# Regrouping the cluster products of an attention and MoE kernel, and moving its preparation work to other steps

## Chip, cores, metric

One core of a Trainium2 chip. The metric is the device time of one execution in microseconds (us), as the median of several executions; for one core there is no second die to compare, and every execution used here was with a granted TensorE clock of 0.994 to 1.0. The timed figure is about 1.9 us above the span of the profile of the same execution (311.12 beside 309.24 us). The one profile of the kernel before is of an execution of 311.12 us. Engines are named as in the profile: PE is TensorE (PEld its weight loads), DVE is VectorE, ACT is ScalarE, POOL is GpSimd, SP is SyncE.

## The reference

Attention over 4 batches x 8 heads x 768 positions x 64, in which a query sees only the keys of its own cluster, and then an MLP on the 3072 x 512 result:

```python
q_assign = argmax(einsum('bhsd,hcd->bhsc', q_n, c_n))     # 16 clusters for each head
k_assign = argmax(einsum('bhsd,hcd->bhsc', k_n, c_n))
scores = where(q_assign == k_assign, scale * q @ k.T, -1e9)
x = softmax(scores) @ v                                   # then to [3072, 512]
h = x @ w_in                                              # [3072, 2048]
g = h + sin(alpha * h)**2 / (alpha + 1e-9)
out = g @ w_out                                           # [3072, 512]
```

## The kernel before

Two heads make a "pair"; a batch has four pairs, and the 16 pairs are numbered through. A batch's attention has 48 steps. Each step issues one score block (`scores`), its exponential on ScalarE (`expo`), and, two or three steps behind, one block of probabilities times v (`pv`). Two PSUM areas hold the scores, so TensorE can be one block ahead of ScalarE and no more. One PSUM bank (OB) collects `pv`; at a pair's sixth block of a head VectorE normalises it, and the next `pv` has to wait for that.

The mask is made by one-hot rows that stand below q and k in the score matmul. For them TensorE forms, for each pair, the cluster scores (the *cluster product*, line 222), and VectorE makes the one-hot rows out of it in four pieces; DMAs on SP's queue put them in place:

```python
def prep_asn(m, part=0, parts=1, bk=None):        # the cluster product of pair m, float32
    ...
    for g in range(4):
        nc.tensor.matmul(
            out=s["asn"][32 * g : 32 * g + 32, ...],   # 32 columns of the array each
            lhsT=cnB[:, 2 * hp + g // 2, :],
            rhs=s["T32"][:, g, ...], start=True, stop=True)

def hot_steps(m, a):
    asn_at.add(a)
    at(a, lambda: (prep_asn(m), prep_hot(m, 0)))  # piece 0: 32x32 transposes out of PSUM
    at(a + 1, lambda: prep_hot(m, 1))             # 1: maximum of each 16
    at(a + 2, lambda: prep_hot(m, 2))             # 2: is_equal
    at(a + 3, lambda: (prep_hot(m, 3), prep_move(m)))   # 3: transposes back; 8 or 4 DMAs
```

Everything that is not attention's own work hangs in a plan by step. In batch 0 that is a lot: `prep_T` (three float32 transpositions on TensorE and a copy, four groups for each pair), `prep_D` (VectorE transposes for later pairs), `x_T` (transposition of a finished pair's result), casts and loads on GpSimd. In batches 1 to 3 the output matmuls of the batch before ("fillers") are dealt out over the steps:

```python
ahead = b == 0 and r % NJ == 1        # plan work goes ahead of pv at these steps of batch 0
if ahead:
    for fn in plan.get(i, []): fn()
for d in due.get(r, []): pv(base + d)
if not ahead:
    for fn in plan.get(i, []): fn()
if fill:
    fill.go((2 if r % NJ == 2 else 0 if r % NJ == 3 else 1) - (i in asn_at))
```

After the 48 steps comes the batch's MLP: for each of 16 blocks `hidden_mm` on TensorE into one of three PSUM areas, `snake` (sine on ScalarE, square on ScalarE or VectorE, multiply-add on VectorE into gT), and the first output matmuls with a lag of some blocks. `hidden_mm` of block f needs the area that `snake` of block f - 3 has read.

The softmax here doesn't subtract the row's maximum and nothing guards it: scores larger than these inputs give would overflow.

## Time and profile before

| | before |
|---|---|
| time, median of the first 3 runs | 312.74 us (311.97 to 312.76) |
| span of the profile | 309.2 us |
| TensorE busy | 300.7 us, 97% |
| ScalarE, VectorE, GpSimd busy | 238.8, 209.7, 141.1 us |
| cluster products | 15 of 8 matmul records, 120 records |

TensorE is nearly always busy, so a wait is not the usual cost here. What counts is how far apart the *starts* of its instructions lie: a duration in the timeline includes the pipeline's drain and overlaps the next one. For ScalarE, likewise, I give the period from one exponential's start to the next; "the period at step n" ends with the exponential of step n. It is 0.71 us when ScalarE is the bound; a longer one tells that TensorE was late with the scores.

### The profile page before, as it was taken

The numbers are of one execution on the slowest core, as the hardware profiler recorded it, in microseconds if no ns is written. First come the engines' busy times: TensorE is split into PE (matmuls) and PEld (weight loads), VectorE is DVE, ScalarE is ACT, GpSimd is POOL, SyncE is SP. The second block draws the span as 40 slices with busy tenths as digits, with TensorE's granted clock in tenths as the row PEclk, the third lists the DMA queues.
The fourth block names the chain that finished last, engine by engine and source line by source line (L and its number), as shares of the span: only waits on it lengthen the run. The fifth ranks groups of instructions, "written<-read, shape, count | busy, mean of one in ns | idle before, by whom it ended". The sixth has DMA issues, their size and how long they took to land.

```text
span 309.2 us, 7194 instructions
## 1 busy us (share of the span) xinstructions
PE 300.7 (97%) x2726; PEld 177.2 (57%) x2726; DVE 209.7 (68%) x369; ACT 238.8 (77%) x323; POOL 141.1 (46%) x231
## 2 busy tenths in 40 slices
PE   7899999999999999999999999999999999999995
PEld 3567666455455665555556656555556666555544
DVE  4786685899769876677867877677935313677721
ACT  5689987976598988687689998688679999687300
POOL 5789978048177199993006089970001090000000
PEclk9999999999999999999999999999999999999999
DMA  7548999999585477981054477420011021000031
GB/s 226 156 160 264 315 228 220 218 196 318 108 200 171 91 190 151 314 295 51 2 141 112 84 177 161 117 85 2 0 68 50 36 47 41 36 0 2 0 136 68
DMA packets 31105, 40.48 MB, mean 131 GB/s; under 512 B 5904, under 2 KB 24928, under 8 KB 31072
## 3 DMA queue, kind: packets, MB, share of 16 engines
q0 software_dynamic: 10240, 21.11, 26.3%
q1 hardware_dynamic: 20592, 18.87, 23.0%
q8 instruction: 21, 0.34, 0.5%
q14 instruction: 12, 0.10, 0.1%
q10 hardware_dynamic: 240, 0.06, 0.1%
HBM read 27.30 MB, written 6.29 MB: 109 GB/s over the span
## 4 chain that ended last, share of the span: by engine, by line
PE 90%; ACT 5%; DVE 3%; issue 1%; DMA 1%; SPq 0%; ACTq 0%; DVEq 0%
PE M L406 20%; PE S L437 18%; PE S L338 13%; PE OB L353 11%; PE M L437 8%; PE S L339 6%; PE OB L406 5%; PE M L222 3%; ACT pT L344 3%; PE S L406 2%; PE M L144 2%; DVE gT L462 1%; PE S L513 1%; DMA QK<-ohT 1%; PE M L377 1%
## 5 line engine op out<-in xcount | busy, mean ns | idle before, releaser
L344 ACT ACTIVATE pT<-S 128x768 bf16<-128x768 f32 x192 | 143.0, 810 | 16.7 <-PE S L339 15.6
L406 PE MATMUL M<-w_out_bf,gT 128*128 128x512 bf16 (+1 forms) x288 | 90.6, 373 | 0.0
L338 PE MATMUL S<-QK 80*128 80x512 bf16 x192 | 72.9, 380 | 2.1 <-ACT pT L344 1.3
L437 PEld LDWEIGHTS <-w_in_bf 128*128 128x128 bf16 x512 | 49.4, 98 | 38.4 <-issue 2.1
L353 PEld LDWEIGHTS <-pT 128*128 128x128 bf16 x1152 | 56.0, 97 | 21.7 <-DVE xs L365 0.7
L437 PE MATMUL S<-xT,w_in_bf 128*128 128x512 bf16 x352 | 66.2, 326 | 0.6 <-DVE gT L462 0.4
L353 PE MATMUL OB<-VX,pT 128*128 128x65 bf16 x1152 | 61.3, 193 | 0.3 <-DVE xs L365 0.3
L199 POOL TENSOR_SCALAR QK<-T 64x384 bf16<-64x384 f32 x80 | 43.4, 542 | 34.3 <-DMA T<-Tq 29.2
L450 ACT ACTIVATE s_sb<-S,alpha_col 128x768 bf16<-128x768 f32 (+2 forms) x45 | 39.7, 886 | 23.5 <-PE S L437 15.7
L406 PEld LDWEIGHTS <-gT 128*128 128x128 bf16 x400 | 39.0, 98 | 31.7 <-issue 6.5
L462 DVE SCALAR_TENSOR_TENSOR gT<-u_sb,ralpha,S 128x768 bf16<-128x768 bf16 (+2 forms) x45 | 44.7, 996 | 11.1 <-ACT u_sb L455 8.2
L339 PE MATMUL S<-QK 80*128 80x256 bf16 x192 | 51.9, 270 | 0.0
L399 POOL DMA_DIRECT2D xT<-xq x48 | 25.8, 546 | 28.2 <-DVE xq L391 27.2
L437 PE MATMUL M<-xT,w_in_bf 128*128 128x512 bf16 (+1 forms) x160 | 30.6, 326 | 0.0
L339 PEld LDWEIGHTS <-QK 80*128 80x128 bf16 x192 | 18.8, 98 | 17.6 <-issue 2.8
L458 DVE TENSOR_TENSOR u_sb<-s_sb 128x768 bf16<-128x768 bf16 (+2 forms) x41 | 23.9, 584 | 6.4 <-ACT s_sb L450 6.4
L211 POOL CAST VX<-v 128x768 bf16<-128x768 f32 x16 | 13.7, 855 | 31.6 <-issue 28.3
L364 DVE RECIPROCAL rec<-OB 128x6 f32<-128x6 f32 x32 | 6.1, 191 | 29.9 <-PE OB L353 29.9
L406 PE MATMUL OB<-w_out_bf,gT 128*128 128x512 bf16 (+1 forms) x80 | 26.2, 358 | 0.0
L450 ACT ACTIVATE s_sb<-M,alpha_col 128x512 bf16<-128x512 f32 (+1 forms) x40 | 20.9, 574 | 6.7 <-PE M L437 6.6
L462 DVE SCALAR_TENSOR_TENSOR gT<-u_sb,ralpha,M 128x512 bf16<-128x512 bf16 (+1 forms) x40 | 22.8, 611 | 4.8 <-ACT u_sb L455 4.4
L338 PEld LDWEIGHTS <-QK 80*128 80x128 bf16 x192 | 18.6, 97 | 6.8 <-issue 2.5
(84 smaller groups left out, 277.4 us busy)
## 6 DMA issues: line engine op xcount, KB each, us to landing
T<-Tq SPq DMA_DIRECT2D x80, 96.0 KB, 2.4
out_dram<-o_sb SPq DMA_DIRECT2D x23, 256.0 KB, 2.1
v<-in_v_dram POOLq DMA_DIRECT2D x14, 384.0 KB, 4.8
q<-in_q_dram POOLq DMA_DIRECT2D x13, 384.0 KB, 6.6
k<-in_k_dram POOLq DMA_DIRECT2D x13, 384.0 KB, 7.1
w_in_bf<-in_moe_w_in_dram POOLq DMA_DIRECT2D x4, 512.0 KB, 10.5
w_out_bf<-in_moe_w_out_dram POOLq DMA_DIRECT2D x4, 512.0 KB, 11.6
xT<-xq POOLq DMA_DIRECT2D x48, 24.0 KB, 2.2
```

What stands on the lines that cost most here:

```text
L199: nc.gpsimd.tensor_scalar(out=QK[0:D, m % NQK, h, t].rearrange("c (n i a) -> c i n a", i=4, a=32)[:, 2 * par : 2 * par + 2], in0=src[:, t] ...
L211: nc.gpsimd.tensor_copy(out=VX[m % NVX][:, :, :, 0:D], in_=st[m]["v32"])
L338: nc.tensor.matmul(out=dst[:, 0:512], lhsT=lhsT, rhs=T[:, 0, 0:512], start=True, stop=True)
L339: nc.tensor.matmul(out=dst[:, 512:S], lhsT=lhsT, rhs=T[:, 0, 512:S], start=True, stop=True)
L344: nc.scalar.activation(out=pT, in_=area(i)[:, 0:S], func=ACTF.Exp, scale=escale)
L353: nc.tensor.matmul(out=o3[:, j, :], lhsT=pT[:, P * j : P * j + P], rhs=VX[m % NVX][:, h, jof(m // NHP, kt), :], start=(kt == 0 and j == 0) ...
L399: nc.gpsimd.dma_start(out=xT[32 * g : 32 * g + 32, 0:2, QS * i : QS * i + QS], in_=xq[0].rearrange("p (h g n) -> p h g n", h=2, g=4)[32 * ...
L406: nc.tensor.matmul(out=bk[:, lo:hi], lhsT=gT[:, f, P * mt : P * mt + P], rhs=w_out_bf[:, f, lo:hi], start=(f == 0), stop=(f == NF - 1),)
L437: nc.tensor.matmul(out=ar[lo // 512][:, 0 : hi - lo] if isinstance(ar, tuple) else ar[:, lo:hi], lhsT=lhsT, rhs=xT[:, kk, :].rearrange("c ...
L450: nc.scalar.activation(out=s_sb[:, lo:hi], in_=src, func=ACTF.Sin, scale=alpha_col[:, f : f + 1])
L458: nc.vector.tensor_tensor(out=u_sb[:, lo:hi], in0=s_sb[:, lo:hi], in1=s_sb[:, lo:hi], op=ALU.mult)
L462: nc.vector.scalar_tensor_tensor(out=gT[:, f, lo:hi], in0=u_sb[:, lo:hi], scalar=ralpha[:, f : f + 1], in1=src, op0=ALU.mult, op1=ALU.add,)
```

## The change

It keeps every instruction and moves them. Neighbouring cluster products stand back to back (7-8, 10-11, 12-13, 14-15, and 4-5 in batch 0's MLP), the one-hot pieces of the second product of each late pair are put at steps where they come after the normalisation, batch 0's transpositions are spread anew, and GpSimd's v cast of pair 2 goes ahead of pair 3's second cast.

```diff
+    def hot_two(m, a, steps):
+        asn_at[a] = 2
+        at(a, lambda: (prep_asn(m), prep_asn(m + 1), prep_hot(m, 0), prep_hot(m + 1, 0)))
+        for n, (i, j, k) in enumerate(((a + 1, a + 2, a + 3), steps)):
+            at(i, lambda n=n: prep_hot(m + n, 1))
+            at(j, lambda n=n: prep_hot(m + n, 2))
+            at(k, lambda n=n: (prep_hot(m + n, 3), prep_move(m + n)))
 ...
-        (3, ((0, 14), (2, 16), (1, 17), (3, 18)), 20, (17, 19)),
-        (4, ((0, 22), (1, 24), (2, 28), (3, 30)), 32, (25, 31)),
-        (5, ((0, 34), (1, 36), (2, 40), (3, 41)), None, (37, 42)),
+        (3, ((0, 11), (1, 14), (2, 16), (3, 18)), 20, (16, 19)),
+        (4, ((0, 22), (1, 23), (2, 28), (3, 34)), None, (25, 35)),
+        (5, ((0, 32), (1, 38), (2, 40), (3, 42)), None, (39, 43)),
 ...
-    for g, i in enumerate((35, 37, 38, 39)):          # prep_D of pair 6
+    for g, i in enumerate((36, 39, 41, 41)):
-    for g, i in enumerate((42, 43, 44, 45)):          # prep_D of pair 7
+    for g, i in enumerate((44, 44, 46, 46)):
 ...
+    hot_one(6, ASTEPS + 8)
+    hot_one(9, ASTEPS + 32)
+    for m, b, r, steps in (
+        (7, 1, 20, (25, 26, 31)),
+        (10, 2, 2, (7, 8, 10)),
+        (12, 2, 32, (38, 41, 42)),
+        (14, 3, 2, (7, 8, 10)),
+    ):
+        hot_two(m, ASTEPS * b + r, [ASTEPS * b + i for i in steps])
 ...
-                at((23, 29, 46)[m], lambda m=m: x_T(m))
+                at((26, 30, 44)[m], lambda m=m: x_T(m))
 ...
-        own = [(1, OB, 3 if b else 4), (0, M0, 5 if b else 6)]
+        own = [(1, OB, 3 if b else 4), (0, M0, 5 if b else 7)]
 ...
+            if b == 0 and f == 1:
+                prep_asn(NHP, bk=OB)
+                prep_asn(NHP + 1, bk=M0)
+                prep_hot(NHP, 0)
 ... (the other one-hot pieces of pairs 4 and 5 after blocks 3 to 9; loads and casts of v)
```

More of the change, by code (lines that the diff above doesn't have):

```diff
@@ L575, in at, with hot_one @@
         plan.setdefault(i, []).append(fn)
-    asn_at = set()
-    def hot_steps(m, a):
-        asn_at.add(a)
+    asn_at = {}
+    def hot_one(m, a):
+        asn_at[a] = 1
         at(a, lambda: (prep_asn(m), prep_hot(m, 0)))
@@ L584, in hot_steps @@
         at(a + 3, lambda: (prep_hot(m, 3), prep_move(m)))
+    def hot_two(m, a, steps):
+        asn_at[a] = 2
+        at(
+            a,
+            lambda: (
+                prep_asn(m),
+                prep_asn(m + 1),
+                prep_hot(m, 0),
+                prep_hot(m + 1, 0),
+            ),
+        )
+        for n, (i, j, k) in enumerate(((a + 1, a + 2, a + 3), steps)):
+            at(i, lambda n=n: prep_hot(m + n, 1))
+            at(j, lambda n=n: prep_hot(m + n, 2))
+            at(k, lambda n=n: (prep_hot(m + n, 3), prep_move(m + n)))
     def pair_steps(m, make, asn, cast):
@@ L602, in prep_new @@
         at(k0 + 17, lambda: prep_cast(m, 1))
-        hot_steps(m, k0 + 8)
     for m, make, asn, cast in (
@@ L619 @@
         at(ASTEPS + 4 + 2 * h, lambda h=h: prep_cast(NHP + 3, h))
-    hot_steps(NHP + 2, ASTEPS + 8)
-    hot_steps(NHP + 3, ASTEPS + 14)
     for m, i in {4: 10, 5: 12, 6: 18, 7: 22}.items():
@@ L640 @@
                     at(2 * ASTEPS - 1, lambda m=m: load_qk(m, eng=nc.gpsimd))
+    hot_one(6, ASTEPS + 8)
[7 more added lines that the diff above has]
+        hot_two(m, ASTEPS * b + r, [ASTEPS * b + i for i in steps])
     for m in range(1, NP):
         if m > 1:
-            at(max(0, STEPS * m - (14 if m < 5 else 26)), lambda m=m: load_v(m, nc.gpsimd))
-        at(max(0, STEPS * m - (5 if m < 5 else 8)), lambda m=m: prep_v(m))
+            at(max(0, STEPS * m - (14 if m < 3 or m == 4 else 19 if m == 3 else 26)), lambda m=m: load_v(m, nc.gpsimd))
+        at(max(0, STEPS * m - (6 if m == 2 else 5 if m < 5 else 8)), lambda m=m: prep_v(m))
     for m in range(NP):
@@ L712 @@
             if fill:
-                fill.go((2 if r % NJ == 2 else 0 if r % NJ == 3 else 1) - (i in asn_at))
+                fill.go((2 if r % NJ == 2 else 0 if r % NJ == 3 else 1) - asn_at.get(i, 0))
         last = NHP * (b + 1) - 1
@@ L734 @@
                 fill.go(10 if f == 2 else 64, "act")
-            if b == 0 and f == 2:
-                prep_asn(NHP + 1, bk=M0)
-            if b == 0 and f in (6, 10):
-                prep_S(NHP + 2 + (f - 6) // 4)
-            if b == 0 and f in (3, 5, 7, 9):
-                prep_hot(NHP + 1, (f - 3) // 2)
-            if b == 0 and f == 9:
-                prep_move(NHP + 1)
+            if b == 0 and f in (5, 8):
+                prep_S(NHP + 2 + (f - 5) // 3)
+            if b == 0 and 3 <= f < 10:
+                m, piece = ((5, 0), (4, 1), (4, 2), (4, 3), (5, 1), (5, 2), (5, 3))[f - 3]
+                prep_hot(m, piece)
+                if piece == 3:
+                    prep_move(m)
             if b == 0 and f == 8:
```

## The prediction

> **What bounds the kernel now.** I read the page first (busy shares, chain), then the busy time by stage, then the TensorE timeline around single cluster products, then the waits. "Step" means one of the 48 score blocks of a batch; "cluster product" is the float32 matmul group of line 222 that gives the cluster scores of one pair of heads.
>
> ```profile
> PE 300.7 (97%) x2726; PEld 177.2 (57%) x2726; DVE 209.7 (68%) x369; ACT 238.8 (77%) x323; POOL 141.1 (46%) x231
> PE 90%; ACT 5%; DVE 3%; issue 1%; DMA 1%; SPq 0%; ACTq 0%; DVEq 0%
> ```
>
> TensorE is busy 97% of 309.2 us and carries 90% of the chain that ended last. So time is won where TensorE gets less to do, or where one of its few waits goes. The busy table by stage (stretch, length, busy time of each engine) says where those waits are:
>
> ```profile
> 11.06:50.87 39.81, 37.89 (x481) 26.17 (x482) 29.81 (x62) 36.69 (x49) 33.84 (x45) 1.00 0.90 236
> 50.87:83.23 32.36, 31.80 (x192) 17.12 (x190) 25.84 (x42) 23.08 (x31) 13.90 (x23) 1.00 0.95 216
> 83.23:121.66 38.43, 38.38 (x466) 22.69 (x465) 30.54 (x58) 34.35 (x47) 25.83 (x46) 1.00 0.65 157
> 154.80:192.35 37.55, 37.55 (x459) 22.64 (x458) 27.87 (x53) 34.31 (x47) 17.98 (x32) 1.00 0.57 134
> ```
>
> The first row is attention of batch 0: TensorE lacks 1.9 us there and ScalarE is busy 36.7 of 39.8 us, so the two hand over to each other. The second is the MLP of batch 0 (0.56 us idle). From 83 us on TensorE has no idle time at all: there only less TensorE time counts, and TensorE time is a matter of start-to-start distances. The TensorE timeline around one cluster product (start, duration, line):
>
> ```profile
> 88.44 0.27 PE L339 MATMUL S<-QK 80*128 80x256 bf16 x1
> 88.64 0.85 PE L222 MATMUL M<-T,cnB 128*32 128x384 f32 x8
> 89.43 0.39 PE L406 MATMUL M<-w_out_bf,gT 128*128 128x512 bf16 x1
> 89.66 0.38 PE L338 MATMUL S<-QK 80*128 80x512 bf16 x1
> ```
>
> A 256-column score matmul is elsewhere followed after 0.11 us; here the product starts 0.20 us after it, lasts 0.79 us to the next start, and the 512-column matmul after it takes 0.23 instead of 0.215 us. One product thus costs 0.09 + 0.79 + 0.01 = 0.89 us. Its eight records start in two bursts of four (7 ns apart within a burst), the second 0.345 us after the first, and the next instruction only 0.44 us after the second burst. So the productive part is 2 x 0.345 = 0.69 us, and 0.20 us is paid for going in and coming out.
>
> **What the Trainium skill says.** "TensorEngine Tiling (Array Packing)", section Key Properties: changing the tiling mode, not merely the tile, drains TensorE. The product's operands are 128*32 (four column tiles) between 128*128 neighbours, and the extra 0.09 us going in and 0.10 us coming out agree. "TensorE: Matmul & The Clock Gate", Part 3, says that column tiles run concurrently, with starts about 4 ns apart; the trace has 6 to 7 ns. "FP8 and Floating Point Precision", section TensorE Precision Notes: true float32 takes four passes; 4 x 384 columns in 0.69 us, two passes to each burst, fit. "PSUM — Partial Sum Buffer", section Engine vs sequencer instructions, calls the VectorE queue strict FIFO: a one-hot piece put ahead of something urgent delays it, as the wait at 43.57 us below shows.
>
> **The change part by part.** The number of instructions of each kind is unchanged; the order listing shows moves only.
>
> (1) Attention of batches 1 to 3. Products 7-8, 10-11, 12-13, 14-15 now stand back to back, each pair in another PSUM bank: four entries and exits vanish, 4 x 0.20 = 0.80 us. Product 10 (at 108.3 us) also went in 0.09 us slower than the rest (0.30 instead of 0.20), and that goes with its merging: about 0.9 us in all. The filler output matmuls give up two places at such a step and are caught up elsewhere, which is neutral. All of it is on the path, since TensorE has no idle time there.
>
> (2) Attention of batch 0. Exponentials cannot follow each other faster than 0.71 us (measured starts). A step's TensorE work is scores 0.325 us plus 0.178 us per probability-times-v block; steps with number 2 modulo 6 have none of the latter, those with 3 have two, the rest one. A transposition group (0.36 us) or an x transposition (0.34 us) is thus hidden at class 2 (0.68) and exposed elsewhere (0.86, measured periods 0.85 to 0.87), at about 0.15 us. Of the 15 such groups after step 10, the kernel before has 14 exposed (only that at step 14 hides); the new one has 10 (14, 26, 32, 38, 44 hide): 4 x 0.15 = 0.6 us. Product 4 leaves step 32, whose period was 1.08 us: 0.37 us. And one wait should go:
>
> ```profile
> 42.74 0.38 PE L338 MATMUL S<-QK 80*128 80x512 bf16 x1 [0.27 <-ACT pT L344]
> 42.95 0.27 PE L339 MATMUL S<-QK 80*128 80x256 bf16 x1
> 43.57 0.54 PE L353 MATMUL OB<-VX,pT 128*128 128x65 bf16 x12 [0.35 <-DVE xs L365]
> ```
>
> TensorE stood at 43.2 us because VectorE's normalisation was queued behind preparation pieces at step 37, which is a step where plan work goes ahead of the product with v. The new plan puts nothing on steps 31, 37 and 43. The period there was 1.21 instead of 0.74 us; I count 0.4 us. Sum 0.6 + 0.37 + 0.4 = 1.4 us. I take off 0.3 for new waits (transposition of pair 3 at step 11, only some 0.4 us after its q landed at 20.44 us; VectorE then ahead of the normalisation of step 13): 1.1 us.
>
> (3) MLP of batch 0. Product 4 is added ahead of product 5, merged: one entry and exit is spared, so it adds 0.89 - 0.20 = 0.69 us to TensorE.
>
> ```profile
> 54.99 0.85 PE L222 MATMUL M<-T,cnB 128*32 128x384 f32 x8
> 56.27 2.83 PE L437 MATMUL S<-xT,w_in_bf 128*128 128x512 bf16 x16 [0.43 <-DVE gT L462]
> ```
>
> After product 5, TensorE waits for the first gT piece: 56.27 - 54.99 = 1.28 us instead of 0.79, so 0.5 us is free and the net is 0.2 us. VectorE gets four more one-hot pieces of about 0.5 us each into blocks 3 to 9. Its work there, from start-to-start times: 0.93 to 1.15 us for an odd block, 1.57 to 1.7 for an even one, seven pieces at 0.49, in all 12.2 us; TensorE's is 1.3 + 3 x 1.52 + 3 x 1.73 = 11.1 us. So VectorE is longer by about 1.1 us, of which the lead of 0.4 to 0.9 us that gT has over its reuse from block 8 on absorbs most: I count 0.25 us of new TensorE waits. One output matmul (lag 7 instead of 6) moves out of a wait into the full tail: 0.2 us. Loss 0.65 us.
>
> (4) The v cast of pair 2 ahead of pair 3's second cast: in the trace that cast ended at 32.96 us and its first reader started after 33.5 us, so it held up nothing; I count 0.
>
> Sum: -0.9 - 1.1 + 0.65 = -1.35 us; 312.74 - 1.35 = 311.4 us. I shade it to 311.3, as the merging removes a sure TensorE cost.
>
> **Rivals.** A: VectorE becomes the bound in the MLP of batch 0 (11.1 us of TensorE against 12.2 us of VectorE in seven blocks): the loss there grows to 1.5 us or more and the total is about 312.3. For it: the loop from TensorE over ScalarE and VectorE back was already tight in blocks 3 to 7 (a wait of 0.29 us at 62.4 us). Against it: the lead from block 8 on. B: the merged pair keeps TensorE from scores for 1.58 us, ScalarE stands idle, and the handover loses what the merge gained; then part 1 gives nothing and the total is 312.2. Against it: after single products, too, ScalarE idles (0.62 us before the exponential at 90.24) while TensorE never does. C: the drain is not paid per mode change but per PSUM bank or stop flag, so that the merged second product still costs 0.89 us: total 312.3. Against it: the interval inside a product, between bursts, carries no such cost; but no row shows two products in succession. D: the rearranged batch 0 works fully and waits fall to almost none: total 310.
>
> **Range and chances.** The parts have errors of about 0.3, 0.6 and 0.6 us, in quadrature 0.9; repeated runs lie 0.8 us apart. So 311.3, with 8 in 10 between 310.1 and 312.7. Over 2% would be 6.3 us, more than all waits of TensorE together, so within 2% is nearly certain (0.98).
>
> **What would show it.** Right: line 222 still 120 matmuls, in four places after 80 us 16 records long with about 1.5 us to the next start; attention of batch 1 and 2 shorter by 0.2 to 0.5 us each, of batch 3 by 0.2; TensorE idle in 11 to 50 us down by over 0.8 us; the wait for xs at 43 us gone. Wrong: TensorE idle of over 0.7 us in blocks 3 to 10 of the first MLP released by gT; entries of 0.3 us or a 0.44 us distance between the two products of a pair; waits for q at step 11; TensorE waiting for xs in later batches.

## The result, and the profile after

The first measurement gave 310.18 us (310.0 to 310.34, 4 runs) beside 312.41 us for the kernel before: ratio 0.9929, 95% interval 0.9911 to 0.9947. The changed kernel was measured twice more, as a mark for the experiments: 0.9933 (interval 0.9898 to 0.9968) and 0.9933 (0.9918 to 0.9949), with medians of 310.22 and 310.03 beside 311.92 and 312.02. A ratio is the mean time of one kernel's runs over that of the other's of the same rounds, so it is not quite the ratio of the medians. The change takes 1.7 to 2.2 us off; 1.4 was predicted. What was set down for the two repeats, in their order:

> The changed kernel once more, on the chip of the runs beside it, so that its parts are compared with it under the same conditions. If the parts add (late pairs alone and batch 0 alone took 0.8 and 0.9 us off the median), 1.7 us off the kernel before: ratio 0.9946. If the two parts help each other, 2.2 us as in the first measurement: 0.993.

> The changed kernel a third time, as the mark for the three runs beside it on the same chip. Ratio 0.993 to the kernel before, as twice already; attention of batch 0 at 37.6 us, or 37.9 if a transposition there waits for its q or k again.

Measured: a ratio of 0.9933 in both, so what the change gives is 0.7% in all three measurements. The first repeat does not decide between its two forecasts: the medians differ by 1.70 us, and the ratio is moved by one run of the kernel before (315.54 us); without that run it would be 0.994.

Where it went is read from the traces by two kinds of mark, the exponentials and the score blocks:

| stage | before | after | difference |
|---|---|---|---|
| attention 0: first exponential's start to the 48th's end | 39.24 | 37.56 | -1.68 |
| MLP 0: from there to the second score block of batch 1 | 32.41 | 33.47 | +1.06 |
| from there to the end | 226.02 | 224.93 | -1.09 |
| sum | | | -1.71 |
| start of the first exponential | 11.58 | 12.48 | +0.90 |

The last row is the start-up, whose instructions are the same; over all profiles it lies between 11.43 and 12.48 us whatever the kernel, so it is left out of comparisons. For that reason the two spans (309.2 and 308.4 us) tell less than the stages. Of the second and third row, 0.22 us is one filler that now runs in the MLP's last part instead of later: it lengthens the one row and shortens the other.

The busy table of the changed kernel by stage (stretch in us, its length, busy time of PE, PEld, DVE, ACT and POOL, clock, DMA share, GB/s), over stretches that answer to the four shown of before:

```profile
11.96:50.09 38.13, 37.23 (x472) 26.37 (x473) 26.99 (x57) 35.90 (x49) 33.02 (x44) 1.00 0.90 242
50.09:83.51 33.42, 32.84 (x200) 17.46 (x199) 27.70 (x46) 23.15 (x31) 15.19 (x26) 1.00 0.99 221
83.51:120.92 37.41, 37.41 (x458) 22.80 (x457) 27.89 (x54) 34.34 (x47) 22.73 (x41) 1.00 0.64 152
153.63:190.83 37.20, 37.12 (x459) 22.97 (x458) 27.29 (x54) 34.32 (x47) 17.36 (x32) 1.00 0.56 132
```

TensorE's lack in attention of batch 0 fell from 1.9 to 0.9 us; in the later batches TensorE is still all but without a pause (37.12 of 37.20 us in the last row), in less time. The TensorE timeline (start, duration, line) shows a merged pair, 7 and 8:

```profile
98.17 0.27 PE L339 MATMUL S<-QK 80*128 80x256 bf16 x1
98.37 1.50 PE L222 MATMUL M<-T,cnB 128*32 128x384 f32 x16
99.80 0.39 PE L338 MATMUL S<-QK 80*128 80x512 bf16 x1
100.02 0.27 PE L339 MATMUL S<-QK 80*128 80x256 bf16 x1
```

Sixteen records, 1.43 us to the next start, with 0.09 us more than usual going in and 0.01 after: 1.53 us, against 2 x 0.89 = 1.78 for two singles. A merged pair spares 0.25 us. The start times of the records show why: within the pair the bursts begin 0.347, 0.322 and 0.322 us apart, and only the last is followed by 0.44 us. The second product has no entry or exit of its own.

In attention of batch 0 the steps around number 40, where TensorE used to wait for xs:

```profile
42.74 0.38 PE L338 MATMUL S<-QK 80*128 80x512 bf16 x1
42.96 0.27 PE L339 MATMUL S<-QK 80*128 80x256 bf16 x1
43.07 0.53 PE L353 MATMUL OB<-VX,pT 128*128 128x65 bf16 x12
43.45 0.38 PE L338 MATMUL S<-QK 80*128 80x512 bf16 x1
```

The twelve products with v start 0.11 us after the scores, where before it was 0.62 us. The periods of the exponentials say the same of the whole stage:

```
step        18   19   20   21   24   25   29   31   33   35   36   40   42   47
before    .873 .873 .708 1.08 .850 .874 .863 .873 1.08 .855 .708 1.21 .873 .844
after     .707 .745 .707 1.20 .872 .707 .869 .738 .737 .863 .707 .706 .707 .737
```

The steps left out changed by 0.05 us or less, but for step 30 (.852 to .707); step 21, with product 3, is the one that got clearly longer.

And in batch 0's MLP, product 4 and 5 together, then the waits:

```profile
53.98 0.85 PE L222 MATMUL OB<-T,cnB 128*32 128x384 f32 x8
54.65 0.83 PE L222 MATMUL M<-T,cnB 128*32 128x384 f32 x8
55.41 0.50 PE L437 MATMUL M<-xT,w_in_bf 128*128 128x512 bf16 x2
55.75 2.76 PE L437 MATMUL S<-xT,w_in_bf 128*128 128x512 bf16 x16
...
61.42 0.38 PE L406 MATMUL OB<-w_out_bf,gT 128*128 128x512 bf16 x1
62.17 0.48 PE L437 MATMUL S<-xT,w_in_bf 128*128 128x512 bf16 x2 [0.37 <-DVE gT L462]
...
78.18 0.38 PE L406 MATMUL M<-w_out_bf,gT 128*128 128x512 bf16 x1
78.77 0.59 PE L406 MATMUL M<-w_out_bf,gT 128*128 128x512 bf16 x2 [0.20 <-DVE gT L462]
```

The wait of 0.43 us ahead of block 3 is filled, as intended. Block 7 (the line at 62.17) has a longer wait ahead of it than before (0.53 us against 0.29), but only because one output matmul of 0.22 us no longer stands in it: counted from the last exponential's end, block 7 starts 0.25 us later than before, exactly as block 3 does. In the tail (the output matmuls after block 15) a filler waits for a PSUM bank that VectorE still reads: the start distance to the filler is 0.59 us, against 0.31 us before and 0.22 us without a wait. The 0.28 us more come from one VectorE instruction, the square of line 458, before and after:

```profile
74.03 0.55 DVE L458 TENSOR_TENSOR u_sb<-s_sb 128x768 bf16<-128x768 bf16 x1
73.60 0.83 DVE L458 TENSOR_TENSOR u_sb<-s_sb 128x768 bf16<-128x768 bf16 x1
```

In all 14 profiles the 419 such squares with which no GpSimd cast of line 199 overlaps took 0.51 to 0.56 us; of the 127 with an overlap 80 took over 0.6 us, up to 1.21. In the changed kernel this square begins 0.08 us after such a cast began, and VectorE has no pause from there to the tail. In e4, with batch 0's MLP as before, it took 0.55 us and the tail was as short as before; in e9 it took 0.85 us and the tail was 0.31 us longer, though the lag was 6. That the cast slows the square is read from these times; no run moved the cast alone.

### The profile page after: what moved, and what is told of

Its sections match the earlier page's. It is cut to its first block, busy times and chain, and to the rows that moved or that the text cites. A ratio compares the mean times of both kernels' runs of the same rounds, so it can differ in the third digit from the quotient of the medians.

```text
span 308.4 us, 7196 instructions
## 1 busy us (share of the span) xinstructions
PE 300.7 (97%) x2726; PEld 178.2 (58%) x2726; DVE 206.2 (67%) x369; ACT 238.2 (77%) x323; POOL 139.6 (45%) x231
## 4 chain that ended last, share of the span: by engine, by line
PE 80%; ACT 10%; DVE 5%; DMA 2%; issue 1%; SPq 0%; DVEq 0%; ACTq 0%
PE M L406 18%; PE S L437 16%; PE S L338 11%; ACT pT L344 10%; PE OB L353 9%; PE M L437 7%; PE S L339 5%; PE OB L406 4%; PE M L222 3%; DVE gT L462 3%; PE S L406 2%; DMA QK<-ohT 2%; PE M L144 2%; DVE u_sb L458 1%; PE S L513 1%
## 5 line engine op out<-in xcount | busy, mean ns | idle before, releaser
L406 PE MATMUL M<-w_out_bf,gT 128*128 128x512 bf16 (+1 forms) x288 | 89.6, 373 | 0.2 <-DVE gT L462 0.2
L199 POOL TENSOR_SCALAR QK<-T 64x384 bf16<-64x384 f32 x80 | 42.0, 526 | 38.6 <-DMA T<-Tq 33.7
L458 DVE TENSOR_TENSOR u_sb<-s_sb 128x768 bf16<-128x768 bf16 (+2 forms) x41 | 23.1, 566 | 6.1 <-ACT s_sb L450 6.1
```

The source lines that it names most:

```text
L199: nc.gpsimd.tensor_scalar(out=QK[0:D, m % NQK, h, t].rearrange("c (n i a) -> c i n a", i=4, a=32)[:, 2 * par : 2 * par + 2], in0=src[:, t] ...
L406: nc.tensor.matmul(out=bk[:, lo:hi], lhsT=gT[:, f, P * mt : P * mt + P], rhs=w_out_bf[:, f, lo:hi], start=(f == 0), stop=(f == NF - 1),)
L458: nc.vector.tensor_tensor(out=u_sb[:, lo:hi], in0=s_sb[:, lo:hi], in1=s_sb[:, lo:hi], op=ALU.mult)
```

## Experiments

All were correct, each with 5 rounds against the kernel before on the same chip (one for e1 to e4, one for e3b, e5 and e6, one for e7 to e9). The three stages are those of the table above; they come from one profile of each kernel.

| kernel | median us | ratio to before | attention 0 | MLP 0 | rest |
|---|---|---|---|---|---|
| before (its one profile) | 311.9 to 312.4 | 1 | 39.24 | 32.41 | 226.02 |
| changed | 310.18, 310.22, 310.03 | 0.9929, 0.9933, 0.9933 | 37.56, 37.88, 37.56 | 33.47, 33.48, 33.47 | 224.93, 225.21, 225.01 |
| e1 late pairs only | 311.19 | 0.9974 | 39.38 | 32.42 | 225.25 |
| e2 batch 0 only | 311.11 | 0.9977 | 37.93 | 33.48 | 225.71 |
| e3 pairs parted | 311.90 | 0.9995 | 37.56 | 33.47 | 226.85 |
| e3b pairs parted, fillers even | 311.58 | 0.9981 | 37.56 | 33.47 | 226.73 |
| e4 product 4 back at step 32 | 309.99 | 0.9936 | 38.43 | 32.50 | 225.73 |
| e5 one-hot of pair 5 later | 312.36 | 1.0005 | 37.56 | 33.47 | 227.33 |
| e6 VectorE transposes back | 310.41 | 0.9945 | 38.16 | 33.51 | 224.96 |
| e7 v cast back | 310.92 | 0.9965 | 37.64 | 33.47 | 224.97 |
| e8 two more in pairs | 310.29 | 0.9944 | 37.85 | 33.50 | 225.11 |
| e9 product 4 at step 44 | 309.82 | 0.9931 | 37.96 | 32.82 | 225.19 |

The 95% intervals are 0.9962 to 0.9986 for e1, 0.9962 to 0.9992 for e2, 0.9982 to 1.0008 for e3, 0.9923 to 0.9949 for e4; they are about 0.0016 either way for e8 and e9 and 0.0034 to 0.0038 for e3b, e5, e6 and e7. So 0.5 us between two medians is not much, and the stages decide where they can.

**e1: the late pairs alone.** The kernel before, with `hot_two` for 7-8, 10-11, 12-13 and 14-15 and nothing of batch 0.

```diff
-        hot_steps(m, k0 + 8)                     # and those of pairs 6 and 7
+    hot_one(6, ASTEPS + 8); hot_one(9, ASTEPS + 32)
+    for m, b, r, steps in ((7, 1, 20, ...), (10, 2, 2, ...), (12, 2, 32, ...), (14, 3, 2, ...)):
+        hot_two(m, ...)
```

> The kernel before with only the cluster products of batches 1 to 3 regrouped (pairs 7-8, 10-11, 12-13, 14-15); batch 0 untouched. My theory (each merged pair spares TensorE one entry and one exit; single 0.89 us, pair 1.53 us in the trace of the changed kernel): 5 + 4 + 1 singles become 2 singles and 4 pairs, so 8.99 - 7.90 = 1.1 us less from the second score block of batch 1 to the end, and nothing else: 311.3 us beside 312.4, ratio 0.9965. Rival (a pair keeps ScalarE without scores for 1.5 us and the handover gives the gain back): ratio 1.000, with TensorE waits for exponentials after the pairs. Rival (nearly all of the change's gain comes from batch 0): above 0.998.

Measured: 0.9974, 0.8 us off the median, and 0.77 us in the rest of the trace with the two stages of batch 0 unchanged (39.38 and 32.42). The merging pays, and the rival of no gain falls. It pays 0.3 us less than expected. Two exponentials, at step 115 (counted through all batches) and 160, start 0.37 us after their scores end instead of 0.10, and TensorE waits 0.24 us for each; both are in all 12 profiles with the late pairs and in neither before nor e2. They are in e3 and e3b too, where the two products of a pair do not touch, so the products' standing back to back is not what brings them on. The timeline puts one of the two down to a product with v (at 168.53 us) and the other to ScalarE itself (at 236.87 us), so it names no single cause, and why they come with this placement stays open. A smaller part is known: in e1 the pair 12-13 lost 0.09 us, as its second product had to wait for a DMA (more on this at e4).

**e2: batch 0 alone.** The changed kernel with products 6 to 15 single at their old steps.

```diff
-    hot_one(6, ...); hot_one(9, ...); for m, b, r, steps in (...): hot_two(m, ...)
+    for m, a in ((6, 56), (7, 62), (8, 68), (9, 80), (10, 92), (11, 104), (12, 116), (13, 128), (14, 140), (15, 152)):
+        hot_one(m, a)
```

> The changed kernel with the products 6 to 15 single again, at the steps of the kernel before; batch 0 as changed. My theory: attention of batch 0 shorter by 1.7 us (37.6 instead of 39.2 us from the first exponential's start to the 48th's end), MLP of batch 0 longer by about 1.0 us, the rest as before: 0.6 us less, ratio 0.998. If the parts add up, this gain and that of the late pairs alone sum to the 2.2 us measured for both; a remainder of over 0.5 us would be an effect that only both together have. Rival (late merging gives nothing): ratio 0.993 here, as for the whole change.

Measured: 0.9977. The MLP of batch 0 is 1.07 us longer, as in the changed kernel. The attention gained 1.31 us, not 1.68: here one transposition had to wait for its q, as the timeline shows:

```profile
20.53 0.35 PE L353 MATMUL OB<-VX,pT 128*128 128x65 bf16 x6
21.08 0.55 PE L144 MATMUL M<-ident_f,q 128*128 128x128 f32 x3 [0.19 <-DMA q<-in_q_dram]
```

That is the transposition of pair 3 that moved from step 14 to step 11; the step's period was 1.26 instead of 0.89 us. In one of the other profiles (the second of the changed kernel) the k transposition of pair 4, moved from step 24 to 23, waited likewise: its k landed at 31.13 us and it started at 31.18, and the period was 1.19 instead of 0.87 us. Such a wait of about 0.3 us stands in three of the eight profiles with exactly this attention of batch 0, at either place, so the early placement lives on a margin that the DMAs do not always leave. The ratios of e1 and e2 make 0.49% together, the changed kernel 0.67 to 0.71%; with the intervals of the two (0.12 and 0.15 either way) that is no proof of a mutual help, and the stages add up without one: -0.77 from e1, and -0.24 in batch 0 and -0.31 behind it (0.22 of it the filler) from e2, or -1.69 with the 0.37 us of that wait taken off, beside -1.71.

**e3: the pairs parted.** Between the two products of each late pair one filler.

```diff
                 prep_asn(m),
+                filler[0].go(1),
                 prep_asn(m + 1),
```

> The changed kernel, except that in the four late pairs one filler output matmul (128*128, bfloat16, taken from the same batch's stock, so the work is the same) stands between the two products. My theory (drain at each change of tiling): each pair costs an exit and an entry again, 0.25 us, so 1.0 us in all: ratio 0.9961 to the kernel before, with the start of the second product about 0.44 us after the first's last burst plus 0.3 us. Rival (the cost of going out belongs to the first product itself, or to the change of PSUM bank, and merging spares nothing; the gain came from elsewhere): time as the changed kernel, 0.993.

Measured: 0.9995, 1.7 to 1.9 us slower than the changed kernel. The part that the theory names is there. The timeline of the parted pair 7-8:

```profile
97.42 0.85 PE L222 MATMUL M<-T,cnB 128*32 128x384 f32 x8
98.20 0.39 PE L406 MATMUL M<-w_out_bf,gT 128*128 128x512 bf16 x1
98.52 0.85 PE L222 MATMUL M<-T,cnB 128*32 128x384 f32 x8
99.31 0.39 PE L338 MATMUL S<-QK 80*128 80x512 bf16 x1
```

From the first product's start to the score block it takes 1.89 us, against 1.43 merged; 0.216 of the 0.46 us is the filler, 0.24 the new exit and entry (the filler starts 0.44 us after the last burst began, where inside a pair it is 0.32, and the second product 0.32 us after the filler, where a 512-column matmul is otherwise followed after 0.216). Four pairs make 1.0 us. The other 0.8 us is a by-product: with one filler more the fillers changed PSUM banks at another step, and one of them met the bank of an x transposition (TensorE idle 0.80 us at 115.66, released by the copy of xT).

**e3b: the same with the fillers even.** The filler taken at the pair is given back two steps later.

```diff
-        asn_at[a] = 3
+        asn_at[a] = 3; asn_at[a + 2] = 1
```

> As e3_pair_parted, but the filler matmul that stands between the two products is taken back two steps later, so that the filler banks change hands at the same steps as in the changed kernel; the 0.8 us wait of a filler for the copy of x out of its PSUM bank, seen once in e3_pair_parted, should not come. Drain theory: four pairs at 0.22 to 0.25 us, 0.9 to 1.0 us slower than the changed kernel. Rival (e3_pair_parted was slow for the bank collision alone): within 0.3 us of the changed kernel.

Measured: 0.9981, 1.4 us slower than the changed kernel by the medians, 1.5 to 1.8 us in the rest of the trace. The bank collision is gone and the four exits and entries are there (distances of 0.44 and 0.32 us at each pair, 1.0 us in all). What remains is my experiment's own: two steps after each pair there is no filler, TensorE's step then has only scores and one product with v, and it waits about 0.2 us for ScalarE. So an entry and an exit are paid wherever the product meets a matmul of the other form, by the distances; the medians of e3 and e3b overstate it, each for a known reason. The filler differs from the product in tiling and in number type, and these two runs do not part them. The traces of the two main kernels help: float32 transposition groups with operands of 128*128 follow a bfloat16 score matmul after 0.108 to 0.109 us like any other, and are followed after 0.109, the distance inside the group. So float32 alone brings no such cost there; a bfloat16 product of the 128*32 form was not run.

**e4: product 4 back in the attention.** The MLP of batch 0 is as before, product 4 is at step 32.

```diff
-        (4, ((0, 22), (1, 23), (2, 28), (3, 34)), None, (25, 35)),
+        (4, ((0, 22), (1, 23), (2, 28), (3, 30)), 32, (25, 35)),
-        own = [..., (0, M0, 5 if b else 7)]
+        own = [..., (0, M0, 5 if b else 6)]       # and the one-hot pieces of pair 5 alone
```

> The changed kernel with product 4 back at step 32 of batch 0's attention and the MLP of batch 0 (product 5 alone, its one-hot pieces at blocks 3, 5, 7, 9, lag 6) as in the kernel before; the rest of the new placement of batch 0 kept. My theory: the MLP of batch 0 loses the 1.0 us that it had gained in length, attention of batch 0 becomes 0.4 to 0.6 us longer; 0.4 to 0.6 us faster than the changed kernel, ratio 0.991 to the kernel before. Rival (moving product 4 into the MLP pays, as the change intends, since it fills a wait there): 0.2 to 0.5 us slower than the changed kernel, ratio 0.994.

Measured: 0.9936, the same as the changed kernel. The MLP of batch 0 shrank by 0.97 us as I expected, the attention grew by 0.87 instead of 0.4 to 0.6. The period behind product 4 took 0.65 us more, for at step 32 there now stands a transposition as well; the other 0.2 us is the last transposition of pair 4, which the edit also moved, from step 34 to step 30, where an x transposition stands. Both my expectation and the rival's miss: product 4 and its transposition in the other stage neither pay nor cost. The rest of this trace is 0.5 to 0.8 us longer than in the changed kernel's, and 0.62 of that is a wait that has nothing to do with product 4, in the pair 12-13:

```profile
177.02 0.85 PE L222 MATMUL M<-T,cnB 128*32 128x384 f32 x8
178.29 0.85 PE L222 MATMUL M<-T,cnB 128*32 128x384 f32 x8 [0.42 <-DMA T<-Tq]
```

The second product starts 1.27 us after the first instead of 0.67, 0.09 us after a T copy landed (178.20 us). In the ten profiles in which this pair is together, such a wait stands in five (0.62 us here, 0.29 in the second of the changed kernel, 0.09 in e1, 0.07 in e5, 0.05 in e7), each time 0.09 us from the landing of a T copy to the product. So this pair, too, lives on a margin that the DMAs do not always leave.

**e5: fewer pieces for VectorE in the MLP.** Is VectorE the bound there?

```diff
-            if b == 0 and 3 <= f < 10:
+            if b == 0 and 3 <= f < 7:             # without the last three pieces of pair 5
+    at(ASTEPS + 1, lambda: prep_hot(5, 1)); at(ASTEPS + 2, lambda: prep_hot(5, 2))
+    at(ASTEPS + 3, lambda: (prep_hot(5, 3), prep_move(5)))
```

> The changed kernel, with the last three one-hot pieces of pair 5 and its move taken out of blocks 7 to 9 of batch 0's MLP and put into steps 1 to 3 of batch 1, where VectorE has room. Theory that VectorE is the bound late in that MLP (it ran without a pause from 73.6 to 80.7 us and TensorE waited 0.10 us at block 9 and 0.58 us for a bank in the tail): the stretch from the end of batch 0's last exponential to the second score block of batch 1 shrinks from 33.5 to about 33.1 us, 0.4 us in all. Rival (those waits come from product 4 and the lag of 7, not from VectorE's pieces): unchanged within 0.1 us.

Measured: the MLP of batch 0 takes 33.47 us, exactly as with the pieces; the starts of its blocks 3 to 15 agree to 0.01 us. So these three pieces cost nothing, and my theory that they make VectorE the late bound falls, as the rival said. And the kernel became 2.1 us slower in a place that I had not looked at:

```profile
98.01 0.85 PE L222 MATMUL M<-T,cnB 128*32 128x384 f32 x8
100.03 0.85 PE L222 MATMUL M<-T,cnB 128*32 128x384 f32 x8 [1.17 <-DMA T<-Tq]
```

Product 8 waits for its T. The eight one-hot moves of pair 5 now stand on SP's queue ahead of the T copies of pair 8; each holds the queue about 0.64 us, five in all. The last T copy was issued at 97.68 us and landed at 99.94, instead of 92.58 and 97.71 (third profile of the changed kernel). Product 9 then waits too (the last T copy of its pair landed at 110.01 us; the profile puts the wait down to the one-hot moves behind it on the same queue, which landed from 110.21 us on); the two exponentials behind have periods of 3.23 and 2.43 us instead of 1.86 and 1.44, which is the whole loss.

**e6: VectorE's transposes at the old steps.**

```diff
-    for g, i in enumerate((36, 39, 41, 41)):
+    for g, i in enumerate((35, 37, 38, 39)):
-    for g, i in enumerate((44, 44, 46, 46)):
+    for g, i in enumerate((42, 43, 44, 45)):
```

> The changed kernel with the VectorE transposes of pairs 6 and 7 at the steps of the kernel before (35, 37, 38, 39 and 42, 43, 44, 45), two of them again on steps 37 and 43 ahead of the normalisation. My theory (a piece ahead of the normalisation makes TensorE wait for xs): a period of about 1.1 to 1.2 us comes back near step 40, attention of batch 0 takes 0.3 to 0.5 us more than 37.6. Rival (the wait at step 40 came from the two transpositions of pair 5 at steps 36 and 40 and not from the transposes): no difference.

Measured: attention of batch 0 takes 38.16 us, 0.6 more, all of it in one period of 1.34 us at step 46. The VectorE timeline and TensorE's:

```profile
45.81 0.57 DVE L165 STREAM_TRANSPOSE Tq<-q 128x384 f32<-128x384 f32 x1
46.30 0.54 DVE L165 STREAM_TRANSPOSE Tq<-k 128x384 f32<-128x384 f32 x1
46.76 0.16 DVE L364 RECIPROCAL rec<-OB 128x6 f32<-128x6 f32 x1
46.95 0.56 DVE L365 TENSOR_TENSOR xs<-OB,rec 128x384 bf16<-128x384 f32 x1
```

```profile
46.80 0.27 PE L339 MATMUL S<-QK 80*128 80x256 bf16 x1
47.57 0.52 PE L353 MATMUL OB<-VX,pT 128*128 128x65 bf16 x12 [0.49 <-DVE xs L365]
```

A transpose at step 43 is ahead of the normalisation in VectorE's queue, and TensorE waits for xs. The mechanism is the one named; the place is step 43 and not 37, since at 37 the transpositions of pair 5 no longer stand beside it. That fits the view that two kinds of piece together made the wait at step 40, which is half of the rival; the transpositions of pair 5 alone at their old steps were not run. The ratio (0.9945) does not tell this from the changed kernel by itself.

**e7: loads and casts of v as before.**

```diff
-  load_v at STEPS * m - (14 if m < 3 or m == 4 else 19 if m == 3 else 26); prep_v at ... (6 if m == 2 else ...)
+  load_v at STEPS * m - (14 if m < 5 else 26);                            prep_v at ... (5 if m < 5 else 8)
```

> The changed kernel with the loads and casts of v, and the first cast of pair 3, at the steps of the kernel before. My theory (the v cast of pair 2 held up nothing): within 0.2 us of the changed kernel. Rival (moving it ahead is what lets batch 0 run without waits now that the steps are shorter): a wait of TensorE for VX near step 27, 0.3 us or more slower.

Measured: 310.92 us, but its six runs spread from 309.44 to 313.68, so the time decides nothing. In the profile (of the fastest run) the attention of batch 0 takes 37.64 us with the same periods but one (0.78 instead of 0.71 at step 40), and no period near step 27 is longer. No sign that this part does anything.

**e8: two more products in pairs.** 6-7 at step 8 and 8-9 at step 32 of batch 1.

```diff
-    hot_one(6, ASTEPS + 8); hot_one(9, ASTEPS + 32)
-        (7, 1, 20, (25, 26, 31)),
+        (6, 1, 8, (13, 14, 16)),
+        (8, 1, 32, (38, 41, 42)),
```

> The changed kernel with products 6-7 and 8-9 paired in batch 1 (at its steps 8 and 32) instead of 6, 7-8, 9: one single less. Drain theory: one entry and exit less, 0.22 to 0.25 us faster than the changed kernel, in batch 1 alone. Rival (the gain of a pair depends on where it stands): 0 or a loss in batch 1 of 0.2 us or more, with TensorE waiting after the pair.

Measured: no gain (batch 1's attention 37.89 us, beside 37.75 to 37.85). The pairs are as short as the others, and the three periods with products are 0.25 us shorter in sum, as expected, but a new wait eats it:

```profile
98.12 0.15 DVE L364 RECIPROCAL rec<-OB 128x6 f32<-128x6 f32 x1
98.31 0.56 DVE L365 TENSOR_TENSOR xs<-OB,rec 128x384 bf16<-128x384 f32 x1
98.62 0.27 PE L339 MATMUL S<-QK 80*128 80x256 bf16 x1
98.93 0.53 PE L353 MATMUL OB<-VX,pT 128*128 128x65 bf16 x12
```

The product with v starts 0.31 us after the scores instead of 0.11: the normalisation came late in VectorE's queue, behind the transposes of x at 97.27 us. The same happens 19 us later; the two cost 0.39 us. The change's care for the steps of the second product's pieces is what such a pair needs.

**e9: an attempt to beat both.** e8's pairs, product 4 at step 44, the x transposition at 46, lag 6.

```diff
+    at(44, lambda: (prep_asn(NHP), prep_hot(NHP, 0)))
-                at((26, 30, 44)[m], lambda m=m: x_T(m))
+                at((26, 30, 46)[m], lambda m=m: x_T(m))
```

> An attempt to beat both: the two more pairs as above, product 4 back in attention of batch 0 but at step 44, where nothing else then stands (the x transposition goes to step 46), product 5 alone after block 2 of the MLP, lag 6 again, and the k transposition of pair 4 back at step 24. My theory: attention of batch 0 0.5 us longer than in the changed kernel, the MLP 1.0 us shorter, batch 1 0.25 us shorter: 0.7 us faster than the changed kernel, ratio 0.991 to the kernel before. Rival (product 4 costs its whole 0.9 us in the attention wherever it stands, as at step 32 in e4_product4_back): 0.3 us faster.

Measured: 309.82 us, ratio 0.9931. Attention of batch 0 is 0.40 us longer, its MLP 0.65 shorter, batch 1 no shorter (as e8). It is not to be told from the changed kernel.

## Why the prediction was right, and where not

- **The bound and the size.** TensorE's time was the thing to count, and the result lies inside the range, at its lower end in the first measurement. The gain was 1.7 us by the stages and 1.7 to 2.2 by the medians, instead of 1.4. That the sum came out so close is in part luck: part 2 gave 0.6 us more than predicted and part 3 lost 0.4 us more.
- **Part 1, late pairs (-0.9 predicted).** Right in mechanism: e3 shows the exit and entry come back when one matmul of another tiling stands between. The size of one merging was 0.25 us instead of 0.20, as inside a pair the bursts are 0.02 us closer than the prediction's 0.345. Against that stand two late exponentials, 0.24 us each, which were not foreseen. Alone the part gave 0.77 us. One reading was wrong: the product at 108.3 us is number 9, which stays single; number 10 stands at 118.16 us. It did no harm, since 10 went in after 0.296 us as well, and in the changed kernel both go in after about 0.20. And one sign failed: attention of batch 3 was to be 0.2 us shorter and became 0.50 longer (36.48 us from its second score block to its last exponential's end, instead of 35.98), while that of batch 1 became 1.01 shorter and that of batch 2 0.35. The prediction overlooked that products 10 and 14 each move from the end of one batch into the next; their sum is what counts.
- **Part 2, attention of batch 0 (-1.4, less 0.3 for new waits).** Without a new wait the trace has -1.68, with one -1.31 and -1.36, so both halves of that sum were real, the wait only not in every run. The count of hidden and exposed groups held: the periods at steps 19, 25, 31, 33, 40 and 42 fell to ScalarE's pace. e6 shows the wait for xs and its cause. What stood ahead of the normalisation at 42.76 us in the kernel before were two copies out of PSUM and two transposes of q and k, not a one-hot piece as the prediction's citation has it; the queue's order is the same.
- **Part 3, MLP of batch 0 (+0.65).** Mis-sized, with two terms wrong. It measured +1.06. Block 3 starts 0.25 us later relative to the last exponential (predicted 0.2), and a wait at block 9 adds 0.10: the predicted "0.25 us of new TensorE waits" by VectorE was too much for blocks 3 to 10. e5 shows that the pieces after blocks 7 to 9 cost nothing; e9, which has the same pieces without product 4 and with a lag of 6, has the 0.10 us too, and e4, with the old pieces, has not, so it comes with the pieces after blocks 3 to 6. The tail took 0.70 us more where 0.2 was set: with a lag of 7 it holds two output matmuls more (one of its own and one filler, 0.43 us) and the wait for a PSUM bank, 0.27 us more than before, which is the slower square. The filler's 0.22 us comes back later, as it is then missing there.
- **Part 4, the v cast (0).** Nothing in e7's profile speaks against it; its times do not decide.
- **The rivals.** A (VectorE the bound, a loss of 1.5 us or more) falls by the loss of 1.06 us; VectorE does cost 0.10 us at block 9 and 0.27 in the tail. B (ScalarE's starvation gives the gain back) falls by e1: ScalarE does idle 1.05 us after the merged pair, and TensorE is nevertheless without a pause there. C (the cost is paid for each product, PSUM bank or stop flag) falls by the distances inside the pair, whose two products have a bank and a stop flag each. D named the right direction for batch 0, but 310 was reached with a longer MLP beside it.
- **What stays open.** Why two exponentials start late with the late pairs. That the first measurement shows 0.5 us more than the stages do needs no cause: its interval reaches from 1.7 to 2.8 us, and the stages rest on one execution of the kernel before, a fast one.

## What to carry to other kernels

Where an engine is busy 97% of the time, measure the distances between the starts of its instructions: an instruction form that differs from its neighbours may cost a fixed amount going in and out, and putting two of them together spares one of each. Before moving preparation work, ask of each in-order queue (VectorE's and the DMA queue of SyncE) what urgent thing will stand behind it; both lost more here in e5, e6 and e8 (2.3, 0.6 and 0.4 us) than a merged pair gains (0.25). And when a piece of work is moved from one stage to another, measure both stages: product 4's move, with one transposition, won 0.87 us in one and lost 0.97 in the next (e4).

## What the Trainium skill lacked or had wrong

- "TensorEngine Tiling (Array Packing)", Key Properties, says that a change of the tiling mode drains TensorE, and gives no cost. Here it was 0.09 us going into a 128*32 float32 product and about 0.1 us coming out; merging two products spared 0.25 us, and one matmul of another form between them brought 0.24 us back (e3).
- "TensorE: Matmul & The Clock Gate", Part 3, gives starts about 4 ns apart for concurrent tiles; in the traces of both kernels here it was 6 to 7 ns.
- "DMA: Bandwidth & Descriptors" counts sequencer cycles per DMA only for "previous generations" beside trn3; no page has a time, measured on this chip, that one small DMA holds SyncE's queue. It was about 0.64 us for each one-hot move or T copy, so eight moves put ahead delayed the issue of the copies behind by 5.1 us and the last one's landing by 2.2 us (e5).
